# Batch 0's attention loop: preparing pieces at other steps, and three ways of turning a tile instead of two

## The chip, the cores and the metric

The program runs on one core of a Trainium2 chip. The metric is the device time of one execution in microseconds (us); the runs of the kernel before have a median of 759.32 us. "About what a measurement tells from no change" is taken as 1% of that, 7.6 us.

## The reference

Three layers follow each other, over 2 batches of 768 tokens:

```
q_bits = (einsum('bhsd,dk->bhsk', q, proj) > 0)      # 6 bits per token and head: a bucket
scores = where(q_bucket == k_bucket, q @ k.T / 8, -1e9)
attn   = exp(scores - max);  attn /= sum + 1e-9;  x = attn @ v      # 8 heads of 64
u      = x + real(fft(fft(x, tokens), channels))     # layer 2
x      = u + relu(layernorm(u) @ w_ch1) @ w_ch2      # 512 -> 2048 -> 512
theta  = x @ w_theta;  y = w_tok_r @ (x cos theta) + w_tok_i @ (x sin theta)   # layer 3
out    = (x + y) + relu((x + y) @ w_ch)
```

The result has to be near float32, so the kernel splits most operands into a high half and the remainder (a low half), and multiplies three of the four combinations.

## The kernel before, in words

A head pair j (of 4 per batch) has two *stacks*, one per head: a tile `stk` that holds Q and K, their remainders and the bucket patterns, so that one product gives the masked scores. A head has 6 *tiles* of 128 queries by 768 keys; batch 0 has 48 tiles. For each tile TensorE (PE) makes the scores (`attn_S`, 4 matmuls, out `pss`), VectorE (DVE) the negated row maximum `nm`, ScalarE (ACT) the exponentials `p`. Then `p` has to be turned (keys on the partitions), in a high and a low float16 half, and PE multiplies it with the values (`attn_AV`, 18 matmuls, out `pso`). After both heads of a pair are through, `fold` (DVE adds on `fa`, with small `zraw`, `hle`, `hlo`, `hlz` pieces) begins the Fourier transform.

Batch 0's tiles are written out by hand in `attention_first` (L473 to L538): a loop over steps n, 12 steps to a head pair, m = n % 12. Inside it every engine keeps the written order (class `Ordered`, which shows as line L64 in the profile; all else shows as L62). Step n issues the scores of tile n+1, the exponentials of tile n, the maximum of tile n+1; then what turns older tiles. There were two kinds of tile, alternating (`pet='dp'`, L94):

- kind d: GpSimd (POOL) copies `p` to the high half and subtracts for the low one (`attn_split`, engine PL for both); two steps later SyncE (SP) issues a DMA transpose of both halves (`transposed`); the product with V stands in step n+5.
- kind p: one step later PE turns `p` as float32 (`turn_pe`, 6 transposes against `ident` into two PSUM tiles `psm`), ACT copies the high halves and DVE subtracts the low ones (`split_turned`); the product stands in step n+3.

Between them stands `prep(0, j)`, a generator that builds the stacks of the next pair in 11 pieces: loads (SP) of `tt` (Q and K) and `vr` (V); scaling K on POOL and the first bucket bits (PE, DVE); Q into stack 0 (`split_q`: an ACT copy, an SP copy of it, a POOL subtraction) with the other bits; K into stack 0 (`split_k`, the same three); bucket patterns in two halves (ACT, `stk<-psm`); the values (`vv`); then Q, K and two pattern halves for stack 1. The dict `pieces` (L478) says which step takes one. `tt` and `vr` have one buffer, `stk` two.

All that follows the loop (the rest of the transform, the conversion of `w1` and `w2` from 64-bit words, batch 1's attention, the MLP, layer 3) is put in order by a scheduler from priorities that are times written in the table T, and by the times of its own model; the loop before it shifts that order. The conversions are ACT `r`, DVE `r`, ACT `w1h`/`w2h`, POOL `w1l`/`w2l`; batch 1's tiles are split by ACT and POOL and all turned by DMA.

Of the kernel before, what the change touches and what calls it, by code (L numbers as in the profile page):

```python
# [11 lines left out]
F16 = mybir.dt.float16  # L12
# [58 lines left out]
def fused_kernel(ctx, tc, A, out):  # L71
# [15 lines left out]
    def stt(eng, out, in0, in1, op, scale=1.0):  # L87
# [3 lines left out]
        return eng.tensor_tensor(out=out, in0=in0, in1=in1, op=op)  # L91

    T = dict(
        pet='dp', dup=1, c2=0, c0=44, cx=0, wm=6, gf=1, o2=0, xs=1, sb=2, al=[['p', 2], ['p2', 3], ['pt', 3]], cs='v', g0=1,  # L94
        lg=[[0, 2], [2, 4], [4, 6]], ub=2, pace0=1.6, lead=60, f0=60.0, w1=60.0, w1s=1.0, b1=115, pace1=2.6,
        w2=100.0, w2s=1.0, m0=170.0, f1=190.0, th=240.0, m1=290.0, z0=330.0, wt=300.0, n1=16, k1=16, c1=32,
        ne=42, es=150, ld='ss', lc='s', ps=[[0, 3], [0, 5], [1, 0], [1, 5]])
# [375 lines left out]
    def attention_first(pace, after):  # L473

        x_t[0] = mk(x_p, [128, NT, DM], F32, "x")
        N = 8 * NT
        ps, nm, ex, p, p2, tp, pt, o = ({} for _ in range(8))
        pieces = {4: 1, 6: 1, 7: 1, 8: 1, 9: 1, 10: 1, 11: 1, 0: 1, 1: 1, 2: 1, 3: 1}  # L478
        ready = [[] for _ in range(N + 8)]
        new = {}  # L480
        slow = []

        def scores(n):
            if n < N:
# [12 lines left out]

        Ordered.keep = True
        at(0)
        scores(0)  # L500
        nm[0], _ = attn_max(ps[0])
        for n in range(N + 7):
            at(pace * n)
            m, kind = n % 12, lambda i: T["pet"][i % 2] if 0 <= i < N else ""
            if n < N:
                scores(n + 1)
                p[n], e = attn_exp(ps.pop(n), nm[n])
                e = e[1]
            if kind(n - 1) == "p":
                tp[n - 1] = turn_pe(p.pop(n - 1))  # L510
            if n + 1 < N:
                nm[n + 1], x = attn_max(ps[n + 1])
                if n + 1 == T["c1"]:
                    gate["p1"] = [x]
                if n + 1 == T["c0"]:
                    gate["cv"] = [x, e]
            if n - 1 in tp:
                pt[n - 1] = split_turned(tp.pop(n - 1))
            for _ in range(pieces.get(m, 0)):
                j = n // 12 + (m >= 4)  # L520
# [391 lines left out]
    h1, l1, c1, c2 = (ev(k) for k in ("aapap", "p", "p", "p"))  # L912
# [237 lines left out]
```

## Time and profile before

| what | us |
|---|---|
| runs before: median (lowest, highest) | 759.32 (758.41, 765.56) |
| the profiled execution | 759.25 |
| its span in the trace | 757.5 |

The profiled execution has 1.75 us around its span. It lies 0.07 us under the median, so that what is worked out against it holds for the median as well. In the rows below PE, DVE, ACT, POOL and SP are the engines, PEclk is the granted clock of TensorE as a share of full speed, and an arrow in brackets gives the idle time before an instruction and what ended it.

### The profile page before, as it was taken

Reading aid. Unit: us, or ns where it says so; the run is one execution under the profiler, and the core shown is the slowest. Engines: PE = TensorE matmul, PEld = TensorE weight load, DVE = VectorE, ACT = ScalarE, POOL = GpSimd, SP = SyncE. Lnnn points to the kernel's source line nnn. Section 1 sums busy time; section 2 is a strip of 40 time slices with the busy share of each in tenths; the row PEclk is TensorE's granted clock in tenths of the full one; section 3 lists DMA queues with packets and bytes.
Section 4 is the critical chain, followed back from the end, with each engine's and each line's share of the span. In section 5 each row is a group of like instructions: output and inputs, shape, how many; then the busy total and the mean of one; then the engine's idle time right before and its main releaser. Section 6 shows DMA issues by size and latency. Waiting matters only on the chain.

```text
span 757.5 us, 13333 instructions
## 1 busy us (share of the span) xinstructions
PE 672.4 (89%) x5300; PEld 526.5 (70%) x5300; DVE 440.9 (58%) x710; ACT 400.3 (53%) x639; POOL 370.7 (49%) x302
## 2 busy tenths in 40 slices
PE   6979775859397997999989979999999989999997
PEld 2767564647286555786676757587485778998997
DVE  6778879698889855543386782055332266552122
ACT  4787595967588798763322151064325555662010
POOL 4786778697666779776560110033403235841000
PEclk8999997969689998999999989999999999999999
DMA  9685768479687999878650061011003611362202
GB/s 321 150 171 102 167 126 167 94 207 195 184 183 166 228 239 262 158 141 120 114 184 7 5 157 29 1 42 29 1 1 126 201 29 43 110 217 77 84 1 83
DMA packets 151358, 93.19 MB, mean 123 GB/s; under 512 B 126272, under 2 KB 136704, under 8 KB 151296
## 3 DMA queue, kind: packets, MB, share of 16 engines
q1 hardware_dynamic: 149424, 85.87, 48.3%
q0 software_dynamic: 1872, 6.47, 2.4%
q8 instruction: 41, 0.67, 0.4%
q14 instruction: 21, 0.17, 0.1%
HBM read 49.62 MB, written 6.29 MB: 74 GB/s over the span
## 4 chain that ended last, share of the span: by engine, by line
PE 43%; DVE 15%; issue 12%; ACT 11%; POOL 10%; DMA 9%; POOLq 0%; SPq 0%; ACTq 0%; DVEq 0%
PE psm L62 26%; PE psf L62 10%; DMA r<-in_wtok 3%; ACT r L62 3%; DMA pt<-p 2%; POOL p L62 2%; PE pss L64 2%; DVE fa L64 2%; DVE nm L64 2%; POOL w1l L62 2%; ACT stk L64 2%; DVE r L62 2%; PE psm L64 2%; DVE fa L62 1%; DMA r<-in_w 1%
## 5 line engine op out<-in xcount | busy, mean ns | idle before, releaser
L62 PE MATMUL psm<-unT,w1h 128*128 128x256 f16 x768 | 131.9, 276 | 7.9 <-DMA unT<-u 4.5
L62 PE MATMUL psm<-unT,w1l 128*128 128x256 f16 x384 | 105.9, 276 | 0.0
L62 PEld LDWEIGHTS <-w1h 128*128 128x128 f16 (+1 forms) x774 | 75.6, 99 | 24.3 <-issue 11.6
L62 DVE SCALAR_TENSOR_TENSOR r<-r 128x512 uint32<-128x512 uint32 (+1 forms) x64 | 59.0, 923 | 55.3 <-ACT r L62 49.5
L64 PE MATMUL pss<-stk 128*128 128x384 f32 x192 | 51.4, 390 | 26.6 <-ACT p L64 6.7
L62 POOL TENSOR_TENSOR w1l<-r,w1h 128x384 fp32r<-128x384 f32 (+1 forms) x36 | 41.0, 1148 | 58.4 <-ACT w1h L62 58.2
L62 PEld LDWEIGHTS <-hh 128*128 128x128 f16 x384 | 37.2, 99 | 43.1 <-issue 2.7
L62 DVE TENSOR_REDUCE nm<-pss 128x1 f32<-128x768 f32 x48 | 45.1, 950 | 34.9 <-PE pss L62 34.9
L62 ACT ACTIVATE r<-r,chalf 128x512 uint32<-128x512 uint32 (+1 forms) x64 | 46.2, 722 | 33.1 <-DMA r<-in_wtok 17.0
L62 POOL TENSOR_TENSOR p<-p,p 128x768 f16<-128x768 f32 x32 | 55.3, 1731 | 15.9 <-ACT p L62 14.3
L62 DVE SCALAR_TENSOR_TENSOR hl<-psm,hh 128x512 f16<-128x512 f32 x48 | 32.9, 686 | 48.9 <-ACT hh L62 48.8
L62 PE MATMUL psm<-w2l,hh 128*128 128x512 f16 x192 | 61.2, 385 | 0.0
L62 PE MATMUL psm<-w2h,hl 128*128 128x512 f16 x192 | 61.0, 383 | 0.0
L62 PE MATMUL psm<-w2h,hh 128*128 128x512 f16 x192 | 60.5, 382 | 0.0
L62 ACT ACTIVATE hh<-psm 128x512 f16<-128x512 f32 x48 | 28.4, 592 | 57.6 <-PE psm L62 57.5
L62 ACT ACTIVATE p<-pss,nm 128x768 f32<-128x768 f32 x48 | 42.7, 894 | 27.9 <-DVE nm L62 26.4
L62 PE MATMUL pss<-stk 128*128 128x384 f32 x192 | 50.7, 389 | 7.6 <-ACT p L62 6.4
L64 PEld LDWEIGHTS pss<-stk 128*128 128x128 f32 x192 | 34.4, 207 | 31.1 <-ACT p L64 8.2
L64 DVE TENSOR_REDUCE nm<-pss 128x1 f32<-128x768 f32 x48 | 45.5, 950 | 15.7 <-PE pss L64 15.4
L62 PEld LDWEIGHTS pss<-stk 128*128 128x128 f32 x192 | 35.1, 206 | 12.0 <-ACT p L62 8.9
L62 POOL TENSOR_SCALAR nn<-nn 128x512 f32<-128x512 f32 x12 | 7.9, 655 | 71.1 <-ACT nn L62 71.1
L62 PEld LDWEIGHTS <-w1l 128*128 128x128 f16 x384 | 38.0, 99 | 6.5 <-issue 1.8
(297 smaller groups left out, 1682.9 us busy)
## 6 DMA issues: line engine op xcount, KB each, us to landing
r<-in_w SPq DMA_DIRECT2D x32, 512.0 KB, 4.6
r<-in_wtok SPq DMA_DIRECT2D x24, 384.0 KB, 3.8
stk<-stk SPq DMA_DIRECT2D x28, 192.0 KB, 3.3
vr<-in_v SPq DMA_DIRECT2D x8, 390.0 KB, 4.6
tt<-in_qT SPq DMA_DIRECT2D x8, 384.0 KB, 3.6
tt<-in_kT SPq DMA_DIRECT2D x8, 384.0 KB, 4.4
xT<-xs SPq DMA_DIRECT2D x12, 256.0 KB, 2.6
xt<-xT SPq DMA_DIRECT2D x4, 768.0 KB, 5.6
```

What stands on the lines that cost most here:

```text
L62: return fn(*a, **k)
L64: self.last = fn(*a, **k)
```

## The change

The diff has two parts: the kinds of tile become `'dap'`, and the pieces of `prep` get other steps.

```
-        pet='dp', dup=1, ...
+        pet='dap', dup=1, ...
...
-        pieces = {4: 1, 6: 1, 7: 1, 8: 1, 9: 1, 10: 1, 11: 1, 0: 1, 1: 1, 2: 1, 3: 1}
+        pieces = {1: (0,), 2: (0, 1), 4: (0, 1), 5: (1,), 6: (1,), 8: (1,), 9: (1,), 10: (1,), 11: (1,)}
...
-            m, kind = n % 12, lambda i: T["pet"][i % 2] if 0 <= i < N else ""
+            m, kind = n % 12, lambda i: T["pet"][i % 3] if 0 <= i < N else ""
...
-            for _ in range(pieces.get(m, 0)):
-                j = n // 12 + (m >= 4)
+            for later in pieces.get(m, ()):
+                j = n // 12 + later
...
-            if kind(n) == "d":
+            if kind(n) in ("d", "a"):
                 p2[n] = soft_tile("p2")
-                attn_split(p.pop(n), ..., PL, PL)
+                attn_split(p.pop(n), ..., AC if kind(n) == "a" else PL, PL)
-            if kind(n - 2) == "d":
+            if kind(n - 2) in ("d", "a"):
                 pt[n - 2], _ = transposed(p2.pop(n - 2))
-            for i, k in ((n - 5, "d"), (n - 3, "p")):
-                if kind(i) == k:
+            for i, k in ((n - 5, "da"), (n - 3, "p")):
+                if kind(i) and kind(i) in k:
                     av(i)
```

Of 48 tiles there were 24 d and 24 p. Now there are 16 d, 16 of a new kind a (the high half is copied by ACT, the low one subtracted by POOL, and the DMA transposes as for d) and 16 p. The eleven pieces of the next pair stood at m = 4, 6, 7, 8, 9, 10, 11, 0, 1, 2, 3; they stand now at m = 2, 4, 5, 6, 8, 9, 10, 11, 1, 2, 4.

On ACT, in the middle of the second pair, from the exponentials of tile 15 to those of tile 19 (`p`, `pt`, `w1h`, `w1l` are rooms that tiles pass through; an instruction that reads `pss` and `nm` is a tile's exponentials, one that reads `psm` into `stk` is half a bucket pattern, one that reads `tt` is Q or K into a stack). Before:

```order
L64 ACTIVATE p_112<-pss_629,nm_643 128x768
L64 ACTIVATE stk_575<-psm_650,hb_85 64x384 x2
L64 ACTIVATE p_112<-pss_676,nm_682 128x768
L64 ACTIVATE w1l_117<-psm_716 128x384
L64 ACTIVATE w1l_117<-psm_717 128x384
L64 ACTIVATE pt_114<-pss_710,nm_724 128x768
L64 ACTIVATE w1h_116<-pss_759,nm_765 128x768
L64 ACTIVATE pt_114<-psm_791 128x384
L64 ACTIVATE pt_114<-psm_792 128x384
L64 ACTIVATE w1l_117<-pss_785,nm_799 128x768
```

The same stretch on ACT now:

```order
L64 ACTIVATE p_112<-pss_595,nm_601 128x768
L64 ACTIVATE w1l_117<-psm_657 128x384
L64 ACTIVATE w1l_117<-psm_658 128x384
L64 ACTIVATE p_112<-pss_651,nm_665 128x768
L64 ACTIVATE stk_499<-psm_604,hb_85 64x384 x2
L64 ACTIVATE w1h_116<-p_112 128x768
L64 ACTIVATE pt_114<-pss_698,nm_704 128x768
L64 ACTIVATE stk_726<-tt_609 64x768
L64 ACTIVATE w1h_116<-pss_718,nm_724 128x768
L64 ACTIVATE pt_114<-psm_778 128x384
L64 ACTIVATE pt_114<-psm_779 128x384
L64 ACTIVATE stk_726<-tt_609 64x768
```

Between the exponentials of tiles 16 and 18 there stood the copies of one turned tile; now there stand half a bucket pattern, the high half of tile 16 (kind a) and the Q of the next stack.

On POOL at the loop's end, from the split of tile 44 before (45 now) on (`u<-x` is work for the transform, `stk` under L62 a stack of batch 1). Before:

```order
L64 TENSOR_SCALAR w1h_116<-w1l_117 128x768
L64 TENSOR_TENSOR w1h_116<-w1l_117,w1h_116 128x768
L64 TENSOR_SCALAR w1h_116<-p_112 128x768
L62 TENSOR_SCALAR u_2036<-x_191 128x6x64
L62 TENSOR_SCALAR u_2036<-x_191 128x6x128
L62 TENSOR_SCALAR u_2036<-x_191 128x6x63
L62 TENSOR_TENSOR stk_2584<-tt_2556,stk_2584 64x768
L64 TENSOR_TENSOR w1h_116<-p_112,w1h_116 128x768
```

The same place on POOL now:

```order
L64 TENSOR_SCALAR w1h_116<-p_112 128x768
L64 TENSOR_TENSOR w1h_116<-p_112,w1h_116 128x768
L62 TENSOR_SCALAR u_1964<-x_191 128x6x64
L62 TENSOR_SCALAR u_1964<-x_191 128x6x128
L62 TENSOR_SCALAR u_1964<-x_191 128x6x63
L64 TENSOR_TENSOR w1h_116<-p_112,w1h_116 128x768
L62 TENSOR_TENSOR stk_2512<-tt_2484,stk_2512 64x768 x2
```

Tile 46 has lost its copy on POOL, and the stack of batch 1 that stood ahead of its subtraction stands behind it.

Right behind that, on POOL, the first conversions of `w1` and the first splits of batch 1's tiles (those into `p2` and `pt`). Before:

```order
L62 TENSOR_TENSOR p2_113<-p_112,p2_113 128x768
L62 TENSOR_TENSOR w1l_2038<-r64_2039,w1h_2037 128x512
L62 TENSOR_TENSOR w1l_2038<-r64_2046,w1h_2037 128x512
L62 TENSOR_SCALAR u_2036<-x_191 128x6x64
L62 TENSOR_SCALAR u_2036<-x_191 128x6x128
L62 TENSOR_SCALAR u_2036<-x_191 128x6x63
L62 TENSOR_TENSOR w1l_2038<-r64_2053,w1h_2037 128x512
```

The same place on POOL now:

```order
L62 TENSOR_TENSOR w1l_1966<-r64_1967,w1h_1965 128x512
L62 TENSOR_TENSOR w1l_1966<-r64_1974,w1h_1965 128x512
L62 TENSOR_TENSOR w1l_1966<-r64_1981,w1h_1965 128x512
L62 TENSOR_SCALAR u_1964<-x_191 128x6x64
L62 TENSOR_SCALAR u_1964<-x_191 128x6x128
L62 TENSOR_SCALAR u_1964<-x_191 128x6x63
L62 TENSOR_TENSOR pt_114<-p_112,pt_114 128x768
```

The conversions have moved ahead of batch 1's first tile. Further on this stays so: the 16th conversion of `w1` stood behind 12 of batch 1's splits and stands behind 9, the 16th of `w2` behind 26 and now behind 24. On PE, 569 matmuls of batch 0's MLP (384 of its first and 185 of its second layer) stood ahead of the last scores of batch 1; now 645 do (453 and 192).

## Rows read from the trace of the kernel before

**Rows 1.** The table by stretches: from:to in us, length, then busy time and instruction count of PE, PE's weight loads, DVE, ACT and POOL, the granted clock, the share of the DMA engines and GB/s.

```profile
14.70:41.10 26.40, 22.09 (x220) 17.61 (x220) 20.00 (x31) 18.16 (x29) 18.78 (x15) 0.85 0.74 185
41.10:50.20 9.10, 7.54 (x107) 6.37 (x104) 6.69 (x10) 8.70 (x15) 6.37 (x5) 1.00 0.68 130
50.20:62.15 11.95, 9.81 (x106) 7.20 (x104) 11.27 (x16) 6.22 (x11) 9.27 (x8) 0.86 0.89 199
62.15:71.80 9.65, 8.15 (x112) 6.58 (x109) 7.05 (x13) 8.53 (x15) 8.12 (x7) 1.00 0.42 85
...
163.40:222.00 58.60, 44.97 (x353) 37.55 (x353) 51.40 (x75) 42.16 (x66) 39.69 (x28) 0.74 0.75 184
222.00:300.00 78.00, 66.72 (x616) 46.42 (x613) 58.52 (x90) 64.34 (x96) 61.90 (x44) 0.97 1.00 223
300.00:377.80 77.80, 76.65 (x799) 55.34 (x798) 34.32 (x46) 42.78 (x57) 52.96 (x37) 0.96 0.79 138
377.80:444.35 66.55, 60.04 (x416) 44.34 (x414) 49.75 (x132) 19.11 (x37) 16.66 (x21) 0.99 0.28 83
444.35:757.50 313.15, 303.03 (x1820) 250.74 (x1820) 118.08 (x184) 115.53 (x207) 79.57 (x77) 0.99 0.23 69
```

**Rows 2.** ACT's instructions in order of time, around tiles 14 to 19.

```profile
47.28 0.86 ACT L64 ACTIVATE w1l<-psm 128x384 f16<-128x384 f32 x2
48.02 1.16 ACT L64 ACTIVATE stk<-psm,hb 64x384 fp32r<-64x384 f32 x2
49.20 0.90 ACT L64 ACTIVATE p<-pss,nm 128x768 f32<-128x768 f32 x1
...
55.53 0.90 ACT L64 ACTIVATE pt<-pss,nm 128x768 f32<-128x768 f32 x1 [2.62 <-DVE nm L64]
59.43 0.90 ACT L64 ACTIVATE w1h<-pss,nm 128x768 f32<-128x768 f32 x1 [3.00 <-DVE nm L64]
...
60.97 0.91 ACT L64 ACTIVATE w1l<-pss,nm 128x768 f32<-128x768 f32 x1
```

**Rows 3.** DVE's instructions in order of time in the stretch of the fold.

```profile
50.20 0.96 DVE L64 TENSOR_REDUCE nm<-pss 128x1 f32<-128x768 f32 x1 [1.38 <-PE pss L64]
52.08 2.47 DVE L64 TENSOR_TENSOR fa<-x 128x384 f32<-128x384 f32 x2
...
55.34 1.01 DVE L64 TENSOR_TENSOR w1l<-psm,w1l 128x384 f16<-128x384 f32 x2
56.27 2.21 DVE L64 TENSOR_TENSOR fa<-fa 128x384 f32<-128x384 f32 x2
58.40 1.81 DVE L64 TENSOR_REDUCE nm<-pss 128x1 f32<-128x768 f32 x2
```

**Rows 4.** Groups of instructions by line: count, then busy us and mean ns of one, and idle time before them; an ACT copy of a whole tile from SBUF, and POOL's subtraction of one (from the groups over the whole program).

```profile
L62 ACT ACTIVATE p<-p 128x768 f16<-128x768 f32 x20 | 16.7, 838 | 2.8 <-DMA pt<-p 2.8
L62 POOL TENSOR_TENSOR p<-p,p 128x768 f16<-128x768 f32 x32 | 55.3, 1731 | 15.9 <-ACT p L62 14.3 <-DVE nm L62 0.9
```

**Rows 5.** POOL at the loop's end, in order of time, and the last stretch of the chain of waits (start, us, what).

```profile
139.50 0.83 POOL L64 TENSOR_SCALAR w1h<-p 128x768 f16<-128x768 f32 x1 [0.72 <-ACT p L64]
140.29 2.60 POOL L62 TENSOR_SCALAR u<-x 128x384 f32<-128x384 f32 x3
142.98 1.82 POOL L62 TENSOR_TENSOR stk<-tt,stk 64x768 fp32r<-64x768 f32 x1
144.87 1.64 POOL L64 TENSOR_TENSOR w1h<-p,w1h 128x768 f16<-128x768 f32 x1
...
146.54 3.67 DMA w1l<-w1h
...
150.26 0.74 PE pso L64 x18
```

**Rows 6.** ACT's and DVE's last work for tile 47, in order of time.

```profile
146.51 0.87 ACT L64 ACTIVATE w1l<-psm 128x384 f16<-128x384 f32 x2
147.03 1.02 DVE L64 TENSOR_TENSOR w1l<-psm,w1l 128x384 f16<-128x384 f32 x2
```

**Rows 7.** Small and large DVE operations with two inputs in SBUF, and what POOL ran beside them.

```profile
95.41 0.17 DVE L64 TENSOR_TENSOR hlo<-fa,hlo 128x3 fp32r<-128x3 f32 x1
119.25 3.09 DVE L64 TENSOR_TENSOR fa<-fa 128x384 f32<-128x384 f32 x2
125.04 2.55 DVE L62 TENSOR_TENSOR hle<-fa,hle 128x4 fp32r<-128x4 f32 x1
...
92.66 1.64 POOL L64 TENSOR_TENSOR w1h<-p,w1h 128x768 f16<-128x768 f32 x1
96.56 1.82 POOL L64 TENSOR_TENSOR stk<-tt,stk 64x768 fp32r<-64x768 f32 x1 [2.26 <-ACT stk L64]
119.92 2.01 POOL L62 TENSOR_TENSOR stk<-tt,stk 64x768 fp32r<-64x768 f32 x1
124.60 2.19 POOL L62 TENSOR_TENSOR stk<-tt,stk 64x768 fp32r<-64x768 f32 x1
```

**Rows 8.** PE's instructions in order of time shortly before the end of batch 1's attention: the MLP's matmuls, second layer (512 columns) and first (256 columns).

```profile
373.16 0.59 PE L62 MATMUL psm<-w2l,hh 128*128 128x512 f16 x2
373.60 0.59 PE L62 MATMUL psm<-w2h,hl 128*128 128x512 f16 x2
374.03 0.38 PE L62 MATMUL psm<-unT,w1h 128*128 128x256 f16 x2
374.25 0.27 PE L62 MATMUL psm<-unT,w1l 128*128 128x256 f16 x1
374.35 0.38 PE L62 MATMUL psm<-unT,w1h 128*128 128x256 f16 x2
```

**Rows 9.** Who waited for whom between 14.7 and 151 us: us in total, times, longest; the waits of PE for a transposed tile.

```profile
PEld L64 <- DMA w1l<-w1h: 2.5, 3, 1.2
PE pso L64 <- DMA w1l<-w1h: 1.5, 2, 0.9
PEld L64 <- DMA pt<-p: 1.2, 1, 1.2
```

More of the change, by code (lines that the diff above doesn't have):

```diff
@@ L93, in fused_kernel @@
     T = dict(
-        pet='dp', dup=1, c2=0, c0=44, cx=0, wm=6, gf=1, o2=0, xs=1, sb=2, al=[['p', 2], ['p2', 3], ['pt', 3]], cs='v', g0=1,
+        pet='dap', dup=1, c2=0, c0=44, cx=0, wm=6, gf=1, o2=0, xs=1, sb=2, al=[['p', 2], ['p2', 3], ['pt', 3]], cs='v', g0=1,
         lg=[[0, 2], [2, 4], [4, 6]], ub=2, pace0=1.6, lead=60, f0=60.0, w1=60.0, w1s=1.0, b1=115, pace1=2.6,
@@ L518, in attention_first @@
                 pt[n - 1] = split_turned(tp.pop(n - 1))
-            for _ in range(pieces.get(m, 0)):
-                j = n // 12 + (m >= 4)
+            for later in pieces.get(m, ()):
+                j = n // 12 + later
                 if 0 < j < 4:
-                    if m == 4:
+                    if j not in new:
                         new[j] = prep(0, j)
                     next(new[j], None)
-            if kind(n) == "d":
+            if kind(n) in ("d", "a"):
                 p2[n] = soft_tile("p2")
-                attn_split(p.pop(n), p2[n][:, 0].bitcast(F16).rearrange("p (a n) -> p a n", a=2), PL, PL)
-            if kind(n - 2) == "d":
+                attn_split(p.pop(n), p2[n][:, 0].bitcast(F16).rearrange("p (a n) -> p a n", a=2), AC if kind(n) == "a" else PL, PL)
+            if kind(n - 2) in ("d", "a"):
                 pt[n - 2], _ = transposed(p2.pop(n - 2))
-            for i, k in ((n - 5, "d"), (n - 3, "p")):
-                if kind(i) == k:
+            for i, k in ((n - 5, "da"), (n - 3, "p")):
+                if kind(i) and kind(i) in k:
                     av(i)
```

## The prediction

> **What bounds the kernel now.** I read the table by stretches first, to see which engine is full where. Take the second head pair of batch 0's loop, 41.10 to 71.80 us [rows 1]. It falls in two regimes. In its first and last part ACT is busy 8.70 of 9.10 and 8.53 of 9.65 us: ACT sets the pace. In its middle, 50.20 to 62.15, ACT is busy 6.22 of 11.95 while DVE is busy 11.27: DVE sets the pace. ACT's own order in time shows what the regimes are made of [rows 2]: around tiles 14 and 15 exponentials, copies of turned tiles and bucket patterns stand end to end; around tiles 17 and 18 ACT waits 2.62 and 3.00 us for the row maximum. DVE's order says why [rows 3]: the maxima stand behind the fold's adds of 2.47 and 2.21 us. So the pieces of the next stacks crowd where ACT is full and are absent where it idles. The change addresses just that; what counts is how much of ACT's idle time it can use, and what the new kind of tile costs.
>
> Behind the loop, PE is busy 45.0 of 58.6 us, then 66.7 of 78.0: 24.9 us idle up to 300 us. From 300 to 377.8, where batch 1's attention ends, it is busy 76.65 of 77.80, and after 444 us 303 of 313 [rows 1]. So before 300 us the waits of several engines bound the time, after it PE does.
>
> **The loop, step by step.** Per pair (12 tiles) there were 6 turned on PE and are 4: ACT loses two pairs of copies at 0.86 us [rows 2], 1.7 us, and gains four whole-tile copies at 0.84 us [rows 4], 3.4 us. ACT's work per pair goes from 8.70 + 6.22 + 8.53 = 23.45 us [rows 1] to about 25.1. DVE loses two subtractions of 1.0 us a pair, PE two tiles of transposes, and POOL gains two subtractions of 1.7 us and loses two copies of 0.8 [rows 3 to 5]. None of the four gets full by that: 25.1 us of ACT stand against a pair of 30.70 us.
>
> In the fold's stretch (tiles 16 to 19) ACT now has 4 exponentials (3.6 us), half a bucket pattern (1.16), two tile copies (1.7), Q and K of the next stack (1.7) and one turned tile (0.9): 9.0 us in place of 6.22, all under DVE's 11.3. What is left for the two stretches where ACT leads is 25.1 - 9.0 = 16.1 us, in place of 17.2: 1.1 us less. Against that, two things lengthen the fold's stretch: both bucket-bit operations of 0.5 us fall into it where one did, and the subtraction of tile 14 now stands ahead of the fold and waits for two ACT copies behind an exponential. In favour, DVE no longer has to subtract a turned tile between the two halves of the fold. I put these at +0.3 together. A pair with a fold gains 0.8 us. The bounds: if ACT's idle time there shrinks all the way to its share in the other stretches (5%, so 25.1 / 0.95 = 26.4), a pair would gain 4.3 us, which DVE's 11.3 us excludes; 2.0 is as far as I go. If the waits of the fold's stretch simply grow by ACT's added 1.6 us, a pair loses 0.5 after the 1.1. Three pairs: -2.4 us, between -6 and +1.5. The first pair has no fold beside it; there ACT gets more work and the last buckets come earlier: 0, between -1 and +1.
>
> The loads now go out at m = 2, one step behind the last read of `tt` instead of three, and SP keeps its order, so a transpose stands behind them. It is wanted three steps later, and PE waits for transposed tiles only 2.5 + 1.5 + 1.2 us in the whole loop [rows 9]. 32 transposes instead of 24 at the same rate would add 1.7 us, spread over steps in which PE is not the bound: 0, at most +1.7.
>
> The loop's end: the chain goes through tile 46. Its copy on POOL (0.83), the transform's three copies (2.60), a stack of batch 1 (1.82), its subtraction (1.64), its transpose (3.67), its product [rows 5]. Now the stack stands behind the subtraction and the copy is ACT's. That frees up to 2.6 us on this branch, but tile 47 is next: its subtraction on DVE ends at 148.05 [rows 6], and behind it a product of 0.74 would end at 148.8 where tile 46's ends at 151.0; ACT's added copy of 0.84 delays that branch. I take -1.2, between -2.2 and 0.
>
> **The sum.** -2.4 - 1.2 = -3.6 us at the loop's end. What follows starts from the loop's last products, the transform and the MLP, so I let it move as a whole. 759.25 - 3.6 = 755.7 us, and the same against the median.
>
> **What follows moves too.** The scheduler has put conversions ahead of batch 1's tiles, and 69 first-layer and 7 second-layer matmuls of the MLP ahead of batch 1's last scores. At 0.107 us (three from 374.03 to 374.35) and 0.22 us (two from 373.16 to 373.60) [rows 8] that is 7.4 + 1.5 = 8.9 us of PE's work. What it costs is bounded by -8.9 (it all fills idle time and is gone later) and +8.9 (it all delays the end of batch 1's attention, and the transform behind it). I take 0: it can fill holes before 300 us, but is missing as filler from 377.80 to 444.35, where PE is idle 6.5 us already [rows 1].
>
> **The rivals.** First, the holes are filled (faster). For it: 24.9 us of idle PE between 163 and 300 us [rows 1], and weights that are converted earlier, so that the MLP has work to offer. Against it: the granted clock is 0.74 in the first of these stretches, and ACT and POOL, which convert, are no emptier than before. If all 8.9 us go into holes: 755.7 - 8.9 = 746.8 us.
>
> Second, the loop gives its gain back at the port between DVE and POOL. An add of 128x3 took 0.17 us with POOL at rest, one of 128x4 took 2.55 beside a POOL subtraction of 2.19; a pair of fold adds took 3.09 beside one of 2.01, and 2.21 elsewhere [rows 3, 7]. So a DVE operation on two SBUF inputs can wait a POOL instruction out. The small pieces of the second fold ran in a gap of POOL (its subtractions stood at 92.66 and 96.56); the stack's subtractions, which were issued at m = 7 and 8, stand now at m = 5 and 6, beside the fold. Two such hits cost 2 x 2.38 = 4.8 us, a longer pair of adds 0.9: 755.7 + 5.7 = 761.4 us. Against it: maxima and subtractions out of PSUM, most of DVE's work, show no such stretching. (The Trainium skill, "SBUF — State Buffer", on the engine ports, states it as an exclusive lock: a DVE operation with two SBUF inputs and a GpSimd operation that reads SBUF block each other for the whole instruction. The trace agrees with that in the 2.55 us; by that rule alone this rival would be the forecast.)
>
> Third, slower: batch 1's attention ends later. Its last 78 us run on a PE that is 98.5% busy, so work put in front of its last scores pushes its end out one for one; the transform behind it is a chain of DVE and PE from which the rest hangs. The price is the same 8.9 us: 755.7 + 8.9 = 764.6 us, and up to 3.6 more if the loop gains nothing. It decides when PE's idle time between 163 and 300 us does not fall below some 20 us. Against it: the same conversions came earlier, which should start the MLP earlier.
>
> **How the numbers follow.** I give the forecast 0.38 (its own range 751 to 760), the filled holes 0.27, the port 0.17, the delayed attention 0.18. Faster by over 1% (under 751.7) takes most of the second case and a little of the first: 0.31. Slower by over 1% (over 766.9) takes half of the last and a bit of the third: 0.13. That leaves 0.56 within 1%, which is about what a measurement tells from no change. The range goes from the filled holes, 745, to the delayed attention with part of the loop's gain lost, 767.
>
> **What would show it.** Right: the last product of the loop ends near 147.4 instead of 151.0; in the second pair ACT waits some 1.5 us less in the fold's stretch, and the distance from tile 12's to tile 24's maximum is 29.9 instead of 30.7 us. The port: DVE's small adds (`hle`, `hlo`) of 1 us and more in the second fold. The holes: PE's idle time between the loop's end and 300 us under 20 us. The delayed attention: its last product behind 378 us. I would be wrong altogether if the loop's end moved by 8 us or more in either direction: then the pace was not set by ACT and DVE in turn.

## The result, and the profile after

The changed kernel took 769.19 us (median of 4 runs, 766.61 to 770.22), the kernel before beside it 759.54: a ratio of 1.0109 [1.0072, 1.0146]. The forecast was 755.7 us, with a range of 745 to 767. Timed again later, the ratio was 1.0123 [1.0086, 1.0159].

The stretches of the changed kernel's trace (from:to, length, then busy us and count of PE, weight loads, DVE, ACT, POOL, granted clock, DMA share, GB/s). The first four run from the row maximum of tile 0 to 12, 16, 20 and 24, as in [rows 1]; the others are those of [rows 1] too:

```profile
14.34:41.98 27.64, 21.79 (x211) 16.25 (x211) 18.70 (x26) 20.04 (x29) 20.04 (x15) 0.84 0.80 202
41.98:50.13 8.15, 6.86 (x94) 5.70 (x91) 4.75 (x7) 8.02 (x12) 7.74 (x6) 1.00 0.75 149
50.13:64.71 14.58, 10.80 (x108) 6.92 (x106) 12.07 (x18) 7.96 (x14) 8.65 (x6) 0.88 0.82 178
64.71:73.95 9.24, 7.06 (x107) 5.97 (x107) 6.45 (x11) 9.06 (x14) 8.50 (x7) 1.00 0.78 149
...
163.40:222.00 58.60, 41.70 (x303) 35.01 (x304) 49.97 (x70) 42.89 (x69) 40.23 (x28) 0.74 0.74 177
222.00:300.00 78.00, 68.07 (x644) 47.12 (x643) 59.36 (x94) 63.52 (x93) 60.49 (x42) 0.96 0.94 220
300.00:377.80 77.80, 74.23 (x748) 53.97 (x748) 32.69 (x47) 41.83 (x56) 48.66 (x35) 1.00 0.70 129
377.80:444.35 66.55, 63.47 (x509) 47.70 (x510) 43.48 (x97) 17.48 (x31) 23.67 (x27) 0.99 0.34 87
444.35:764.80 320.45, 304.79 (x1818) 251.15 (x1816) 126.48 (x224) 121.03 (x216) 81.44 (x78) 0.97 0.24 72
```

Read the second pair first. The stretches in which ACT leads did get shorter, 9.10 to 8.15 and 9.65 to 9.24 us, with ACT busy 8.02 of 8.15. The stretch of the fold grew from 11.95 to 14.58. (In three further traces of this loop, after_again, a_b1_60 and a_c0_47 below, the three stretches take 8.13 to 8.15, 15.04 to 15.90 and 9.25 to 9.26 us.) [rows 3] has DVE there before; here are SP, PE, POOL and DVE of that stretch now, each in order of time:

```profile
50.05 0.35 SPq L64 DMA_DIRECT2D tt<-in_qT  x1
...
51.40 5.97 SPq L64 DMA_TRANSPOSE w1l<-p  x2
...
54.88 0.80 PE L64 MATMUL psm<-tt,projb 128*32 128x384 f32 x2 [2.78 <-DMA tt<-in_qT]
56.64 1.07 PE L64 MATMUL psm<-tt,projb 128*32 128x384 f32 x2 [0.96 <-POOL tt L64]
...
48.19 1.83 POOL L64 TENSOR_TENSOR stk<-tt,stk 64x768 fp32r<-64x768 f32 x1
...
55.76 0.83 POOL L64 TENSOR_SCALAR tt<-tt 128x768 f32<-128x768 f32 x1 [1.49 <-DMA tt<-in_kT]
...
52.94 2.21 DVE L64 TENSOR_TENSOR fa<-x 128x384 f32<-128x384 f32 x2
55.07 0.94 DVE L64 TENSOR_REDUCE nm<-pss 128x1 f32<-128x768 f32 x1
57.75 0.55 DVE L64 TENSOR_SCALAR bits<-psm 64x384 bf16<-64x384 f32 x1 [1.73 <-PE psm L64]
58.22 2.63 DVE L64 TENSOR_TENSOR fa<-fa 128x384 f32<-128x384 f32 x2
```

The load of the next pair's Q goes out at 50.05 us, 1.15 us earlier than before (51.20), though it was moved two steps ahead: it still waits for the last reader of its one buffer, POOL's subtraction for the stack, which ends at 48.19 + 1.83 = 50.02. PE's projection stands two steps (some 4 us) earlier, so PE waits 2.78 us for Q and then 0.96 for the scaled K, with the next scores behind it in its queue; DVE's bits wait 1.73, and the fold's second half stands behind them. Before, the load went out behind that same reader, and the projection ran at 59.10 us without a wait:

```profile
49.34 1.83 POOL L64 TENSOR_TENSOR stk<-tt,stk 64x768 fp32r<-64x768 f32 x1
...
51.20 0.42 SPq L64 DMA_DIRECT2D tt<-in_qT  x1
...
59.10 1.37 PE L64 MATMUL psm<-tt,projb 128*32 128x384 f32 x4
```

The end of batch 1's attention, its last product, in the trace of before and of after:

```profile
382.46 0.72 PE L62 MATMUL pso<-vv,x 128*128 128x65 f16 x18
```

```profile
394.27 0.72 PE L62 MATMUL pso<-vv,x 128*128 128x65 f16 x18
```

It comes 11.8 us later, the span is 7.3 us longer. In the written order, 528 first-layer MLP matmuls stand ahead of it where 446 did; "ahead" below is this count.

### The profile page after: what moved, and what is told of

The parts are those of the page before. It is cut to its first block, busy times and chain, and to the rows that moved or that the text cites. A ratio compares the mean times of both kernels' runs of the same rounds, so it can differ in the third digit from the quotient of the medians.

```text
span 764.8 us, 13244 instructions
## 1 busy us (share of the span) xinstructions
PE 666.5 (87%) x5252; PEld 518.5 (68%) x5252; DVE 431.0 (56%) x694; ACT 407.4 (53%) x639; POOL 376.7 (49%) x302
## 4 chain that ended last, share of the span: by engine, by line
PE 38%; issue 10%; DMA 7%; POOL 6%; DVE 6%; ACT 4%; POOLq 0%; SPq 0%; DVEq 0%; ACTq 0%
PE psm L62 26%; PE psf L62 9%; DMA r<-in_wtok 3%; DMA x<-p 2%; POOL p L62 2%; ACT r L62 2%; PE pss L62 2%; PE pso L62 1%; DVE u L62 1%; POOL w1l L62 1%; DVE r L62 1%; DMA r<-in_wch 1%; DVE t L62 1%; POOL w2l L62 1%; DVE bs L62 1%
## 5 line engine op out<-in xcount | busy, mean ns | idle before, releaser
L62 PE MATMUL psm<-unT,w1h 128*128 128x256 f16 x768 | 133.0, 277 | 7.2 <-DVE hl L62 5.4
L62 PE MATMUL psm<-unT,w1l 128*128 128x256 f16 x384 | 106.5, 277 | 0.0
L62 PEld LDWEIGHTS <-w1h 128*128 128x128 f16 (+1 forms) x774 | 75.8, 100 | 25.0 <-issue 11.0
L62 DVE SCALAR_TENSOR_TENSOR r<-r 128x512 uint32<-128x512 uint32 (+1 forms) x64 | 53.7, 840 | 66.1 <-ACT r L62 59.0
L64 PE MATMUL pss<-stk 128*128 128x384 f32 x192 | 52.2, 397 | 27.4 <-ACT p L64 7.5
L62 POOL TENSOR_TENSOR w1l<-r,w1h 128x384 fp32r<-128x384 f32 (+1 forms) x36 | 42.8, 1200 | 66.5 <-ACT w1h L62 65.4
L62 ACT ACTIVATE r<-r,chalf 128x512 uint32<-128x512 uint32 (+1 forms) x64 | 46.0, 718 | 39.4 <-DMA r<-in_wtok 16.1
L62 PEld LDWEIGHTS <-hh 128*128 128x128 f16 x384 | 37.1, 98 | 43.8 <-issue 2.7
L62 ACT ACTIVATE hh<-psm 128x512 f16<-128x512 f32 x48 | 28.4, 591 | 71.2 <-PE psm L62 71.2
L62 DVE TENSOR_REDUCE nm<-pss 128x1 f32<-128x768 f32 x48 | 45.2, 950 | 37.2 <-PE pss L62 37.2
L62 ACT ACTIVATE p<-pss,nm 128x768 f32<-128x768 f32 x48 | 42.7, 895 | 40.4 <-DVE nm L62 34.3
L62 PE MATMUL psm<-w2h,hh 128*128 128x512 f16 x192 | 62.1, 384 | 0.0
L62 PE MATMUL psm<-w2l,hh 128*128 128x512 f16 x192 | 61.7, 382 | 0.0
L62 POOL TENSOR_TENSOR p<-p,p 128x768 f16<-128x768 f32 x32 | 54.4, 1703 | 14.3 <-ACT p L62 8.3
L62 PE MATMUL psm<-w2h,hl 128*128 128x512 f16 x192 | 61.4, 382 | 0.0
L62 DVE SCALAR_TENSOR_TENSOR hl<-psm,hh 128x512 f16<-128x512 f32 x48 | 33.0, 688 | 49.2 <-ACT hh L62 49.0
L62 PE MATMUL pss<-stk 128*128 128x384 f32 x192 | 48.1, 374 | 7.0 <-ACT stk L62 3.2
L62 PEld LDWEIGHTS <-w1l 128*128 128x128 f16 x384 | 38.2, 99 | 7.0 <-issue 2.2
L62 POOL TENSOR_SCALAR nn<-nn 128x512 f32<-128x512 f32 x12 | 7.9, 657 | 67.3 <-ACT nn L62 67.3
L62 PEld LDWEIGHTS pss<-stk 128*128 128x128 f32 x192 | 33.4, 197 | 11.0 <-ACT stk L62 4.1
## 6 DMA issues: line engine op xcount, KB each, us to landing
xt<-xT SPq DMA_DIRECT2D x4, 768.0 KB, 4.8
```

The source lines that it names most:

```text
L62: return fn(*a, **k)
L64: self.last = fn(*a, **k)
```

## The experiments

Two theories. *The loop*: the next pair's stack is wanted before it is there, the loop ends later, and the rest follows. *Delayed attention*: the order behind the loop puts more MLP ahead of batch 1's last product, which sets the end. Rivals: the new kinds of tile, or where the bits stand, cost the time themselves. Here is what all runs gave; pairs are distances between the maxima of tiles 0, 12, 24, 36 and 47, times in us. Each trace is one execution: the changed kernel's is the fastest of its four runs (766.61 us), after_again's, the same kernel, the slowest of four (773.29), and their last products lie 3.9 us apart. A difference of that size in the last product or the span of two traces shows nothing by itself.

| run | ratio to before | pairs 1 to 4 | max 47 | ahead | last product | span |
|---|---|---|---|---|---|---|
| before | 1 | 26.34, 30.72, 32.83, 34.58 | 139.2 | 446 | 382.5 | 757.5 |
| changed | 1.0109 [1.0072, 1.0146] | 27.64, 31.97, 32.93, 36.72 | 143.6 | 528 | 394.3 | 764.8 |
| after_again | 1.0123 [1.0086, 1.0159] | 27.67, 32.46, 32.96, 36.71 | 144.7 | 528 | 398.1 | 771.4 |
| e1_pieces | 1.0074 [1.0045, 1.0102] | 27.78, 34.43, 36.31, 33.03 | 145.2 | 467 | 388.6 | 761.3 |
| e2_kinds | 1.0153 [1.0113, 1.0193] | 26.62, 31.46, 32.96, 37.15 | 142.5 | 473 | 399.6 | 771.9 |
| e3_bits_later | 1.0248 [1.0207, 1.0289] | 28.65, 32.96, 41.55, 38.53 | 156.1 | 502 | 406.2 | 777.9 |
| e4_k_earlier | 0.9944 [0.9913, 0.9974] | 27.69, 30.02, 33.26, 34.07 | 138.9 | 488 | 385.5 | 756.5 |
| a_noload | one run, 769.67 us | 27.63, 29.22, 32.93, 36.71 | 141.3 | 528 | 395.4 | 767.9 |
| a_noload_t | 1.0062 [1.0035, 1.0090] | 27.69, 29.24, 32.91, 36.70 | 141.2 | 528 | 395.4 | 768.0 |
| a_nowait | one run, 771.22 us | 26.76, 29.79, 34.84, 33.83 | 139.8 | 502 | 395.2 | 769.4 |
| e5_scale | 1.0051 [1.0019, 1.0084] | 26.47, 33.38, 34.90, 34.10 | 143.1 | 528 | 396.1 | 769.1 |
| a_c0_47 | 1.0010 [0.9982, 1.0038] | 27.67, 32.45, 35.84, 34.86 | 145.2 | 478 | 392.4 | 760.1 |
| a_b1_60 | 1.0056 [1.0019, 1.0094] | 27.66, 33.29, 32.83, 35.59 | 143.9 | 415 | 389.1 | 762.5 |
| b_b1_140 | 1.0150 [1.0103, 1.0197] | 26.43, 30.74, 32.85, 34.62 | 139.0 | 556 | 397.7 | 772.3 |
| e4_b1_60 | 0.9972 [0.9940, 1.0004] | 27.68, 31.06, 33.20, 34.06 | 141.1 | 384 | 382.4 | 757.9 |
| e4_c0_47 | 0.9957 [0.9937, 0.9978] | 27.65, 31.05, 33.26, 32.33 | 138.9 | 469 | 381.0 | 754.6 |

**One half of the change alone.** e1_pieces keeps the two old kinds, e2_kinds the old steps:

```
e1:  -  pet='dap'   T["pet"][i % 3]
     +  pet='dp'    T["pet"][i % 2]
e2:  -  pieces = {1: (0,), 2: (0, 1), 4: (0, 1), 5: (1,), 6: (1,), 8: (1,), 9: (1,), ...}
     +  pieces = {4: (1,), 6: (1,), 7: (1,), 8: (1,), 9: (1,), 10: (1,), 11: (1,), 0: (0,), ...}
```

> The kernel before with the new table of steps alone; tiles alternate as before between the two old kinds. Late load theory (the load two steps earlier stands behind the last scaled K of the pair before, and the bits and projections that wait for it stand ahead of scores and of the fold's second half): the loop keeps what the changed kernel lost, tile 12 to 24 at 31.5 to 32.5 us where before had 30.7, the last maximum of the loop at 142 to 144 us where before had 139.2. Kinds theory (the three kinds cost the time, with GpSimd's and VectorE's shared port): 12 to 24 stays within 0.4 of 30.7. Delayed attention theory for what follows: 467 first-layer MLP matmuls stand ahead of batch 1's last product where before has 446, 21 x 0.107 = 2.2 us later on top of the loop's shift, so a time of 761 to 765 us; if what follows the loop hides all, 759.5.

> The kernel before with the three kinds of tiles alone; the steps of the next stack stand where they stood. Late load theory: nothing is late, and the tiles turned by TensorE keep the gain that the changed kernel showed between fold and fold (0.5 to 0.95 us a pair): 12 to 24 at 29.9 to 30.4 us, last maximum of the loop at 137 to 139. Kinds theory: 12 to 24 at 31.5 or more, and the last maximum at 141 or later. Delayed attention theory: 473 first-layer matmuls ahead of batch 1's last product against 446, 27 x 0.107 = 2.9 us, so 760 to 763 us even where the loop ends 1 to 2 us sooner; if only the loop counts, 757 to 759.

The steps alone lose 3.7 us in the second pair, more than expected: PE waits 2.66 us for Q at 54.17, and POOL 4.44 for K. Its third pair loses another 3.5 us, which nothing had foretold. So much for the late load. But the kinds alone do not gain; the second pair is 31.46 where 29.9 to 30.4 was expected. The load is late there too, on another path. SP's queue and the two that wait, in order of time:

```profile
49.55 5.06 SPq L64 DMA_TRANSPOSE w1l<-p  x2
54.66 1.24 SPq L64 DMA_DIRECT2D tt<-in_qT  x1
...
60.25 0.83 POOL L64 TENSOR_SCALAR tt<-tt 128x768 f32<-128x768 f32 x1 [2.18 <-DMA tt<-in_kT]
...
61.13 0.83 PE L64 MATMUL psm<-tt,projb 128*32 128x384 f32 x2 [1.45 <-POOL tt L64]
```

With three kinds the added transpose stands ahead of the load, which goes out at 54.66 where it went at 51.20 before. Neither half of the change is a gain alone (1.0074 and 1.0153). The 773.5 us of e2 were not expected by any theory (760 to 763 at most).

**Bits later, K earlier.** Both leave the kinds and the load's step.

```
e3:  -  {1: (0,), 2: (0, 1), 4: (0, 1), 5: (1,), 6: (1,), 8: (1,), ...}
     +  {1: (0,), 2: (0, 1), 4: (0,), 5: (1,), 6: (1,), 7: (1,), 8: (1,), ...}
e4:  +  {0: (0,), 2: (0, 1), 4: (0, 1), 5: (1,), 6: (1,), 8: (1,), ...}
```

> The changed kernel with the bits and projections of the next stack one step later (step 5 in place of 4, the following pieces one step on); the load stays at step 2. Late load theory: the load has one step more, 2.5 us, to land, and POOL's scaled K as much, so TensorE's projections wait under 1 us in place of 2.8 and 1.0, and 12 to 24 falls from 32.0 to 30.5 to 31.3 us. Kinds theory: 12 to 24 stays at 31.7 to 32.3. Delayed attention theory: 502 first-layer matmuls ahead of batch 1's last product against 528 in the changed kernel and 446 before: 2.8 us less than the changed kernel from that, 763 to 766 us.

> The changed kernel with one piece, the scaled K and its split of the stack under work, at step 0 in place of step 1, so that the buffer that the next load writes is read for the last time a step sooner; load and bits stand where the change put them (steps 2 and 4). Late load theory: the load goes out up to one step (2.5 us) sooner, the projections' wait of 2.8 us shrinks to under 1.5, and 12 to 24 falls from 32.0 to 30.6 to 31.5 us. If the load's own way is what is late and not its start, or the kinds cost the time, 12 to 24 stays at 31.7 to 32.3. Delayed attention theory: 488 first-layer matmuls ahead of batch 1's last product against 528: 4.3 us less than the changed kernel, 762 to 765 us.

In its loop e4 came out as the late load foretells: the load goes out at 47.94, the first projection waits no more, the second pair takes 30.02 us in place of 31.97, and the kernel is faster than the one before. SP and PE:

```profile
47.94 1.15 SPq L64 DMA_DIRECT2D tt<-in_qT  x1
...
53.42 0.83 PE L64 MATMUL psm<-tt,projb 128*32 128x384 f32 x2
```

The size varies from trace to trace. Two more kernels with e4's loop (e4_b1_60, e4_c0_47) took 31.06 and 31.05 us for this pair, with a wait for the scaled K of 2.05 and 1.81 us; four with the changed loop took 31.97 to 33.29. So the earlier reader gave back 1 to 3 us, and the pair is about as long as before (30.72). The delayed-attention theory had e4 at 762 to 765 us, by its 488 matmuls ahead; it took 757.1, so the count alone does not give the time.

e3 went the other way, and shows a second thing that is late. In the third pair (POOL, then PE):

```profile
90.36 1.95 POOL L64 TENSOR_TENSOR w1h<-w1h 128x768 f16<-128x768 f32 x1
92.28 1.13 POOL L64 TENSOR_SCALAR tt<-tt 128x768 f32<-128x768 f32 x1
...
93.47 1.49 PE L64 MATMUL psm<-tt,projb 128*32 128x384 f32 x2 [3.82 <-POOL tt L64]
```

A step later, the scaling of K stands on POOL behind one tile subtraction more than in the changed kernel, the first line, and PE waits 3.82 us for POOL. That is under half of the 8.6 us that this pair lost; the granted clock from 88 to 112 us was 0.69, and the rest was not taken apart. Later is not safer where the queue in between belongs to the tiles.

**The load, and then the scaling, taken out.** In both, `tt` is filled once.

```
a_noload:  +  if first or b or n == 2:
                  ld.dma_start(out=o, in_=i[b, j])
a_nowait:  -  if not first:
           +  if not first and b:
                  pl_copy(tt[:, 1], tt[:, 1], 0.125)
```

> The changed kernel without the loads of queries and keys for batch 0's second to fourth pair: their tile is filled once and read again, so the last three pairs compute on the first pair's queries and keys; all else is issued as before. Late load theory (what the changed kernel lost in the loop is time in which TensorE and VectorE wait for the new pair's queries and keys): no wait for a DMA is left ahead of the projections, the pairs fall from 31.97, 32.93 and 36.72 us to 29.9 to 30.6, 31 to 32.3 and 34 to 36, and the last maximum from 143.6 to 137 to 140. If the kinds and the shared port cost the time: 12 to 24 stays at 31.7 to 32.3 and the last maximum at 143 or later. If GpSimd's place in its own queue is what is late (scaled K behind the upper halves of the tiles), a wait for GpSimd at the projections stays at 1 us or more in each pair and half of the loss stays.

> Run a_noload with GpSimd's scaling of the keys left out too for batch 0's second to fourth pair, so that nothing new stands between the pair before and TensorE's projections (the last three pairs compute on the first pair's queries and keys, scaled once). In a_noload TensorE still waited 2.43 us for the scaled keys in the second pair, and the first pair was as long as in the changed kernel (27.63 us). Late GpSimd theory (the scaled keys, now at step 4, stand on GpSimd behind a tile's upper half that waits for ScalarE, and TensorE, VectorE's bits and the next maxima wait in turn): first pair 26.2 to 26.8, second 27.7 to 28.8 (29.22 in a_noload), third 31 to 32.5 (32.93). If the bits and projections lose by where they stand, whatever they wait for: first pair 27.3 or more, second 29 or more. The fourth pair, which prepares no stack of batch 0, stays at 36.2 to 37.2 by both.

Without the load the second pair falls by 2.75 us to 29.22, below before's 30.72; the others do not move (27.63, 32.93, 36.71). So the load costs in one pair only. (Without it the DMA engines also carry two transfers of 384 KB less, and PE still waits 2.43 us for the scaled K in that pair.) Without the scaling the first pair falls to 26.76, as expected. The second did not fall further (29.79; expected 27.7 to 28.8), the third rose to 34.84 (expected 31 to 32.5), and the fourth fell by 2.9 us, which no theory had (below). POOL's place in the first pair is confirmed from the other side by e5, which scales K a step sooner:

```
e5:  +  pl_copy(tt[:, 1], tt[:, 1], 0.125);  yield        # and a piece at step 3
```

> Run e4_k_earlier with GpSimd's scaling of the keys as a piece of its own at step 3, a step ahead of the projections and bits. Late GpSimd theory: the first pair's wait of 1.3 us for the scaled keys goes, first pair 26.2 to 27.0 us (27.69 in e4_k_earlier), second 29 to 31 (30.02), since GpSimd may now wait itself for the load. If the first pair's loss isn't from the scaled keys: 27.4 or more. Behind the loop 528 first-layer matmuls ahead of batch 1's last product against 488: 4.3 us later; with a loop 1 us shorter 758 to 763 us by the delayed attention theory, 754 to 757 if the loop alone counts.

First pair 26.47 us. POOL and PE, first of the changed kernel:

```profile
23.72 1.64 POOL L64 TENSOR_TENSOR w1h<-w1h 128x768 f16<-128x768 f32 x1
25.33 0.83 POOL L64 TENSOR_SCALAR tt<-tt 128x768 f32<-128x768 f32 x1
...
26.22 0.83 PE L64 MATMUL psm<-tt,projb 128*32 128x384 f32 x2 [1.33 <-POOL tt L64]
```

and of e5:

```profile
22.43 0.83 POOL L64 TENSOR_SCALAR tt<-tt 128x768 f32<-128x768 f32 x1 [0.86 <-PE pss L64]
...
24.82 0.93 PE L64 MATMUL psm<-tt,projb 128*32 128x384 f32 x4
```

The scaling stood behind a tile's low half; PE's wait is gone with it. In e5's second pair (33.38, expected 29 to 31) POOL itself waits 2.06 us for K at 52.87, with the tiles' work behind it. Its 764.5 us lie above the 758 to 763 expected, on the side of the order behind.

**The loop's end.** The first conversions of `w1` let in after tile 47 instead of 44 (`c0=44` to `c0=47`), in the changed kernel and in e4.

> The changed kernel with the first conversions of w1 let in behind tile 47 of batch 0 in place of tile 44: the six ScalarE instructions of 0.66 to 0.78 us that stood ahead of tile 43's copy, and ahead of the exponentials of tiles 45 and 46, come after the loop. Late tail theory (the fourth pair's 2.1 us are these conversions ahead of the copy that is new on ScalarE, and TensorE's clock falling while it waits): from maximum 44 to 47 7.3 to 8.5 us in place of 10.36 (7.83 before the change), last maximum 140.5 to 142. If the fourth pair loses by the copies on ScalarE themselves: 9.5 or more. Behind the loop 478 first-layer matmuls stand ahead of batch 1's last product in place of 528: 50 x 0.107 = 5.4 us sooner, and with a loop 2 us shorter a time of 762 to 766; if the order behind counts for nothing, 767 to 769.

> Run e4_k_earlier with the first conversions of w1 let in behind tile 47 in place of tile 44. Late tail theory: from maximum 44 to 47 7.3 to 8.2 us in place of 8.42, so at most 1 us sooner. 469 first-layer matmuls ahead of batch 1's last product against 488: 2.0 us sooner. Together 753 to 756 us by the delayed attention theory; 757 or more if the later conversions hold the first layer's matmuls back by as much as they free.

From maximum 44 to 47 it was 7.83 us before and 10.36 in the changed kernel (10.34 to 10.36 in its four traces with and without the load); 8.50 in a_c0_47, 6.67 in e4_c0_47, 8.42 in e4, 8.48 in a_nowait, and 9.22 in a_b1_60 (below), whose loop is the changed kernel's, with the same instructions in the same order here. What differs there is the clock. The scores on PE (4 matmuls) of tiles 45 and 46; of the changed kernel, then of a_b1_60:

```profile
133.57 1.65 PE L64 MATMUL pss<-stk 128*128 128x384 f32 x4 [3.89 <-ACT w1h L64]
138.75 1.65 PE L64 MATMUL pss<-stk 128*128 128x384 f32 x4 [1.52 <-ACT w1l L64]
```

```profile
135.01 1.65 PE L64 MATMUL pss<-stk 128*128 128x384 f32 x4 [3.56 <-ACT w1h L64]
140.19 0.97 PE L64 MATMUL pss<-stk 128*128 128x384 f32 x4 [1.74 <-ACT w1l L64]
```

The mean granted clock of these stretches is 0.56 and 0.82, and 10.36 - 9.22 = 1.14 us are what the lower clock cost. At 0.75 the kernel before took 7.83: the other 1.4 us are the new order of the tail, with the copy on ACT behind the conversions. The conversions themselves cost 1.8 to 1.9 us (10.36 against 8.50, 8.48 against 6.67). That e4 and a_nowait are shorter by another 0.7 us is a matter of where the measure begins: their maximum 44 itself comes later, behind two DVE operations of 1.15 and 1.32 us that took 0.54 and 0.56 in the changed kernel. The granted clock between 136 and 140 us was 0.50 in the changed kernel, then 1.00 before:

```profile
132.00:136.00 4.00, 2.43 (x22) 2.12 (x23) 2.84 (x5) 3.79 (x7) 0.00 (x0) 0.50 0.52 100
136.00:140.00 4.00, 2.48 (x27) 2.31 (x25) 1.61 (x3) 3.48 (x5) 2.02 (x2) 0.50 0.00 0
```

```profile
132.00:136.00 4.00, 3.55 (x28) 3.27 (x28) 3.12 (x5) 4.00 (x8) 0.00 (x0) 0.59 0.20 39
136.00:140.00 4.00, 3.69 (x36) 2.86 (x38) 3.47 (x8) 3.12 (x6) 2.98 (x3) 1.00 0.01 2
```

PE was busy 2.43 of the first 4 us, where before had 3.55. In time, a_c0_47 (761.1 us) is back at before's (1.0010), although the maximum of tile 47 comes 1.6 us later than in the changed kernel (145.2, expected 140.5 to 142; its second and third pairs are 3.4 us longer) and the loop's last product 7 us later. Its order behind has 478 matmuls ahead in place of 528, and the conversions stand elsewhere. e4_c0_47 (757.1) was expected at 753 to 756 and is no faster than e4.

**The order behind the loop alone.** The due time of batch 1's attention, `b1=115`, set to 60 in the changed kernel and in e4, and to 140 in the kernel before; the loop is left alone.

> The changed kernel with the due time of batch 1's attention at 60 in place of 115; the loop is not touched. 415 first-layer MLP matmuls stand ahead of batch 1's last product where the changed kernel has 528 and the kernel before 446. Delayed attention theory (the time behind the loop follows what stands ahead of batch 1's last product): the loop stays as it was in the changed kernel (last maximum 142.5 to 144.5), the last product comes 113 x 0.107 = 12.1 us sooner, near 382, and 371 to 375 us lie behind it, so 755 to 760 us. If the loop alone made the loss: 766 to 770. If the order behind only trades one stage against the other: last product sooner, time within 2 us of 769.

> The kernel before with the due time of batch 1's attention at 140 in place of 115; the loop is not touched. 556 first-layer matmuls ahead of batch 1's last product against 446: 110 x 0.107 = 11.8 us. Delayed attention theory: last maximum of the loop as before (138.5 to 140), last product near 394 against 382.5, and the time 766 to 772 us, a loss of the changed kernel's size with the old loop. If the order behind the loop costs nothing: 759 to 762.

> The changed kernel with the scaled K one step sooner (run e4_k_earlier) and the due time of batch 1's attention at 60 in place of 115. 384 first-layer matmuls ahead of batch 1's last product against 488 there: 104 x 0.107 = 11.1 us. Delayed attention theory: the loop as in e4_k_earlier (last maximum near 139), the last product 11 us sooner than its 385.5, near 375, and a time of 746 to 752 us. If what is moved behind batch 1's attention only comes back later, 755 to 759.

b_b1_140 is the clean one: the loop of before (139.0), 556 matmuls ahead, and 772.3 us against 760.1, a loss of 12.2 us without any change in the loop. Taking the attention ahead gives less: a_b1_60 gained some 4 us over the changed kernel (1.0056 against 1.0109), not 10 to 14, and e4_b1_60 (759.4 us, expected 746 to 752) nothing over e4. Pushing it back cost in full, pulling it ahead did not pay. The traces show part of why. With 113 and 104 matmuls fewer ahead, 12.1 and 11.1 us of work at 0.107 us each, the last product came only 5.2 and 3.1 us sooner: from 200 us to that product PE was idle 24.0 us in a_b1_60 against 22.4 in the changed kernel, and 23.9 in e4_b1_60 against 18.9 in e4, and the mean granted clock was 0.91 against 0.95, and 0.92 against 0.97.

**The loop alone, timed.** a_noload beside the changed kernel on one chip, since a single run could not settle it.

> The changed kernel itself once more, beside the next run on the same chip. Both theories: 1.007 to 1.015 of the kernel before, as at first, so 765.5 to 772 us against 760.4; first pair 27.6 to 27.7 us, since no wait there hangs on a transfer, and the second, which waits for the load, between 31.9 and 33.3 as in the three runs of this loop so far.

> Run a_noload once more, now timed: the changed kernel without the loads of queries and keys for batch 0's second to fourth pair (the last three pairs compute on the first pair's queries and keys). Its loop ends 2 to 4 us sooner than the changed kernel's beside it, by the second pair alone; the order behind is the same, 528 first-layer matmuls ahead of batch 1's last product. If the loop's loss reaches the end: 2 to 4 us faster than the changed kernel beside it. If the order behind sets the end (the delayed attention theory): within 1.5 us of it, and the last product within 2 us of that kernel's.

768.0 us (764.5 to 769.8) against 771.8 (769.4 to 773.3): the loop's 3.5 us (141.2 against 144.7) reach the end, as 3.8. And without the load's wait the kernel is still at 1.0062 [1.0035, 1.0090]. So both theories have a part in the loss of some 9.5 us, but the size of each part is not shown. By this pair of runs about 4 us are the late load; a_nowait, whose loop ended 3.8 us sooner than the changed kernel's, took 771.2 all the same, in one run. The order is worth some 4 us by a_b1_60 and some 7.5 by a_c0_47, with the loop's loss still in both; each figure comes from two comparisons with before, each uncertain by 3 us. These do not add up to one sum.

e2 fits neither theory: 473 matmuls ahead, a loop that ends 3.3 us later than before's, and 12 us lost. From 200 us to its last product (399.6) PE is idle 30.3 us, where before had 19.4. Why is open, so it is not excluded that the new kinds cost something behind the loop by themselves.

## Why the prediction was wrong, point by point

**Two steps failed.** The larger is the term for what follows the loop, "I take 0" (under *What follows* below); the other is the loads. In the trace, an execution of 766.61 us or 10.9 above the forecast, the loop's last product ends 5.3 us later than the 147.4 forecast, and 5.6 more are lost behind it; in after_again's (773.29 us) the two are 6.6 and 11.0.

**The loads.** The step is "The loads now go out at m = 2 ... It is wanted three steps later ... 0, at most +1.7". It was priced as a place in a program. In time the load moved by 1.15 us, since the last reader of the single `tt` (the stack's subtraction on POOL) ended at about the same time (50.02 against 51.17), while the projections moved by some 4 us. They stand two steps behind the load, not three, and at the head of PE's queue. The price was 2.75 us or more in the second pair (31.97 to 33.29 in four traces, 29.22 and 29.24 without the load); the queue of POOL added 0.9 to 1.2 in the first pair (a_nowait, e5), which had been put at 0. That PE waited little for transposed tiles (5.2 us; with the 0.9 of `PE pso` for `pt`, which [rows 9] leave out, 6.1) says nothing of a load behind them.

**ACT's balance was right.** ACT was busy 8.02 + 7.96 + 9.06 = 25.0 us in the second pair (25.1 forecast; 8.0 and not 9.0 of it in the fold's stretch). The stretches in which it leads shrank by 0.95 + 0.41 = 1.36 us (1.1 forecast), and in all four traces of this loop. With the load gone the second pair is 1.5 us shorter than before; with the load there but sooner, in e4's loop, it lies between 0.7 shorter and 0.3 longer (0.8 shorter forecast). The gain in ACT's stretches is real, and the wait hides it.

**The loop's end.** Forecast -1.2 us. The chain through tile 46 did lose about that and more: from the last maximum to the last product 152.7 - 143.6 = 9.1 us where [rows 5] give 151.0 - 139.2 = 11.8. But what stands ahead of it lost 2.5 us, 1.4 by the new order of the tail, with a copy behind conversions, and 1.1 by the clock. The last product came at 152.7, not 147.4.

**What follows** was taken at 0 with +8.9 as a bound, and this term was mis-sized: the order cost 4 to 7.5 us here, by a_b1_60 and a_c0_47 (which moves conversions, too), and 12.2 in b_b1_140. The third rival, delayed attention (chance 0.18, 764.6 us and up to 3.6 more), is the nearest to what happened, with a loop that lost on top, which pushed it over the range. Its sign showed where it was said it would: PE's idle time from 163.4 to 300 us did not fall below 20 but rose from 24.9 to 16.9 + 9.9 = 26.8, so the matmuls that went ahead filled no hole there. Behind 444 us PE now idles 15.7 us where before had 10.1. The text took 377.8 us for the end of batch 1's attention; the last product stands at 382.46.

Two figures of the table bear on this. From the last product to the end of the span it is 370.5 to 375.5 us in all kernels but a_c0_47 (367.7): a later product goes with a later end, to within some 5 us. In the changed kernel 4.5 of its 11.8 us came back behind it (375.0 to 370.5), in b_b1_140 nothing did (374.7). And the way from the loop's last maximum to it grows from 241 to 247 us at 384 to 488 matmuls ahead to 250 to 259 at 502 to 556, except for e2 (257 at 473).

**The port** was a rival at 5.7 us and is there, at a smaller price. DVE and POOL at the end of the third pair, after:

```profile
96.06 1.46 DVE L64 TENSOR_TENSOR hlo<-zraw,hlo 128x189 fp32r<-128x189 f32 x1 [0.43 <-ACT hlo L64]
97.44 0.79 DVE L64 CAST hlo<-fa 128x3 fp32r<-128x3 f32 x1
...
95.48 1.82 POOL L64 TENSOR_TENSOR stk<-tt,stk 64x768 fp32r<-64x768 f32 x1 [3.19 <-ACT stk L64]
97.27 0.94 POOL L64 TENSOR_SCALAR p<-p 128x768 f16<-128x768 f32 x1
```

These two took 0.35 and 0.16 us before, with POOL between two instructions ([rows 7]):

```profile
94.94 0.35 DVE L64 TENSOR_TENSOR hlo<-zraw,hlo 128x189 fp32r<-128x189 f32 x1 [0.43 <-ACT hlo L64]
95.22 0.16 DVE L64 CAST hlo<-fa 128x3 fp32r<-128x3 f32 x1
```

That is 1.7 us, about what the stretch from maximum 28 to 32 grew by (14.56 to 16.18); no run takes the port away by itself. (The Trainium skill, "SBUF — State Buffer", on the engine ports, has a DVE operation with two SBUF inputs and a GpSimd operation that reads SBUF shut each other out for a whole instruction. The trace agrees for the first of the two, which ends at 97.52, 0.2 us after POOL's subtraction.) The prediction's 2.55 us ([rows 7]) outlast the subtraction beside them, which ends at 126.79: they end at 127.59, with POOL's next instruction.

```profile
126.76 0.82 POOL L64 TENSOR_SCALAR p<-pt 128x768 f16<-128x768 f32 x1
```

And its 2.21 us for two adds of the fold "elsewhere" are no price of an undisturbed pair: with POOL mostly idle a pair took 1.23 us (last section).

## What to carry to other kernels

Before a consumer is moved ahead, look for what releases its producer: here the load into a single buffer went out when the last reader was done, two steps ahead in the program or not, and the consumer then waited at the head of an in-order queue with everything behind it. Move the last reader first (e4: one piece one step sooner, and with it 40 matmuls fewer ahead, turned +1.1% into -0.6% [-0.9, -0.3]). And where a scheduler orders what follows, count what its new order puts ahead of the product on which the rest hangs: on an engine as full as PE here that is a term of the sum, not a bound to be set to 0.

## What the runs showed of the hardware that was not expected

The granted clock can make a wait cost more than its length. At the loop's end PE was busy 2.43 of 4 us at 0.50; the next scores took 1.65 us in place of 0.97, and three tiles took 10.36 us at a mean clock of 0.56 against 9.22 at 0.82, with the same instructions of the loop in the same order. What let the clock rise sooner in the second case is not shown.

The fold's adds on DVE depend on what POOL does beside them. Here are two of them in the third pair, of the changed kernel and then of a_c0_47, which has the same pieces and kinds and where DVE's bits waited ahead of them:

```profile
89.03 1.23 DVE L64 TENSOR_TENSOR fa<-fa 128x384 f32<-128x384 f32 x2
...
90.48 1.81 POOL L64 TENSOR_TENSOR stk<-tt,stk 64x768 fp32r<-64x768 f32 x1 [1.22 <-issue]
```

```profile
90.02 0.55 DVE L64 TENSOR_SCALAR bits<-psm 64x384 bf16<-64x384 f32 x1 [1.51 <-PE psm L64]
90.50 2.76 DVE L64 TENSOR_TENSOR fa<-fa 128x384 f32<-128x384 f32 x2
...
90.37 1.89 POOL L64 TENSOR_TENSOR stk<-tt,stk 64x768 fp32r<-64x768 f32 x1 [0.33 <-POOL w1h L64]
```

With POOL idle for most of their time the two adds took 1.23 us, beside its subtraction 2.76. So the 2.47 and 2.21 us of [rows 3], which set the pace of the fold's stretch before the change, are themselves stretched. This, and the wait ahead of the adds, goes with the larger part of the third pair's spread, 32.93 us in the changed kernel and 35.84 in a_c0_47: 1.7 us of the 2.9 come before maximum 31, at much the same mean clock (0.85 and 0.87), and 1.2 behind it, at 1.00 and 0.77.
